# Cutting the first load of a key tile into three, in a one-core attention decode kernel

## The chip, the cores and the metric

The kernel runs on one core of a Trainium2 chip. The metric is the device time of one execution in microseconds (us); lower is better. A run is repeated, and the median is given with the lowest and the highest.

The names in this document are those of the profile. PE is the matrix engine (TensorE), and PEld its weight load. DVE is VectorE, ACT is ScalarE, POOL is GpSimd, SP is SyncE. A small q behind a name (SPq, DVEq) means the engine's sequencer, which issues transfers, waits and branches. The transfers themselves are made by 16 DMA engines that run side by side. Memory on the core (SBUF) has 128 partitions.

## What is computed

One query position attends to 65536 keys. There are 32 query heads and 8 heads of keys and values, so 4 query heads share one head of keys and values.

```python
B, Hq, Hkv, Sq, Sk, D = 1, 32, 8, 1, 65536, 128        # all in bf16
k = jnp.repeat(k, rep, axis=1)                          # rep = 4
v = jnp.repeat(v, rep, axis=1)
scores = jnp.einsum("bhqd,bhkd->bhqk", q, k) * D ** -0.5
p = softmax(scores, axis=-1)
return jnp.einsum("bhqk,bhkd->bhqd", p, v)
```

Keys and values are 268 MB together, and each of their bytes is used once for 4 query heads.

## The kernel before, in words

**Tiles.** A head's 65536 keys are laid on the 128 partitions, 512 rows (keys) to a partition. A row is 128 numbers of 2 bytes, so 256 bytes. A tile is half of a head: `NT = 256` rows in each partition, 64 KB in each partition and 8.4 MB together. There are 32 tiles, 16 of keys and 16 of values. The buffer `buf` holds three of them as a ring.

**Loads.** All tiles come in through SP. The helper `load` (L132, its transfer is on L134) writes one tile, or a part of its rows, into place `at % 3` of the ring, always in all 128 partitions. The order is written out by hand in the list `tiles` (L151 to L154): four tiles of keys, then values, then keys two heads ahead of the values. The first three loads wait for nothing; the first of all (L140) is issued ahead of everything else that SP does, before the start-up barrier that the profile books on L147, and the second on L150 behind it. From the fourth on SP first waits until the place is free (L162 to L167): for a key tile until PE or DVE has passed it, for a value tile until PE has used it. The last value tile comes in eight pieces (`PIECES`), so that little is left to do when the last byte has come. Every load adds 16 to a semaphore of its own place or piece when it has landed, one for each DMA engine. Loads on SP go through one queue, q1 in the profile.

**The query.** ACT loads q (8 KB, L222) through its own queue, q10. DVE transposes it (L298), PE multiplies it (L434), ACT copies it (L224), and POOL spreads it into the weights of the first head (L203).

**Keys.** For each head DVE takes a landed key tile (`turn`, L302; the wait is a `take` of the tile's semaphore, booked on L219) and transposes it in place in four steps (L308). PE multiplies the steps against the query's weights into four banks of scores (L453), with a `clear` (L411) ahead of each bank.

**Values.** DVE takes the maximum of the scores (L358), ACT makes the exponentials (L239), DVE transposes them (L313), and PE multiplies them with the rows of the value tiles (L477). PE runs the tiles as a loop with branches, not as straight code.

**DVE's start.** Before the first tile DVE makes small constant tables out of an identity matrix that POOL writes (L279 to L295): `rep`, `quad`, `sel`, `each`, then `rows4` (L287), then `away` (L292); then it waits for q (L297) and transposes it (L298). The tables and q's transpose are what PE waits for at its first instruction (L433).

**The end.** PE works through the last pieces (L530, L542), ACT scales the result (L252) and stores it.

Of the kernel before, what the change touches and what calls it, by code (L numbers as in the profile page):

```python
# [15 lines left out]
P = 128  # L16
D = 128
NT = 256
# [3 lines left out]
BY = {  # L22
    (G - 2, 0): (NT,), (G - 2, 1): (128, 128), (G - 1, 0): (128, 128),
}
N = 2
FAR = 2.0 ** 126
STEP = 32
# [5 lines left out]
def kernel(  # L33
# [24 lines left out]
    pe, dve, act, pool, sp = nc.tensor, nc.vector, nc.scalar, nc.gpsimd, nc.sync  # L58
    half = NT * D
    ring = 3 * half  # L60

    def sbuf(name, shape, dtype=fp32):
        return nc.alloc_sbuf_tensor(name, list(shape), dtype)
# [4 lines left out]
    buf = sbuf("buf", (P, ring), bf16)  # L68
# [27 lines left out]
    def sem(name):  # L96
        sems.append(nc.alloc_semaphore(name))
        return sems[-1]

    sK = [sem(f"sK{b}") for b in range(3)]  # L100
    sC, sD = sem("sC"), sem("sD")
    sL = [sem(f"sL{x}") for x in range(sum(map(len, BY.values())))]
    sP = [sem(f"sP{x}") for x in range(len(PIECES))]
    sQ = sem("sQ")
    sV = sem("sV")
    kt = sem("kt")
    clr = sem("clr")
# [21 lines left out]
    kr = [k[0, g].rearrange("(p n) d -> p (n d)", p=P) for g in range(G)]  # L129
    vr = [v[0, g].rearrange("(p n) d -> p (n d)", p=P) for g in range(G)]  # L130

    def load(at, src, s, lo=0, n=NT):  # L132
        at = at % 3 * half + lo * D
        return sp.dma_start(  # L134
            out=buf[:, at:at + n * D], in_=src[:, s * half + lo * D:s * half + (lo + n) * D]
        )

    first = load(0, kr[0], 0)  # L140
    tc.no_tile_sem_insts.add(first.ins.name)
    first.then_inc(sK[0], 16)
    tc.add_to_no_dep_group("first", first.ins)
    tc.declare_fence(pool.nop().ins, group="first")
    home = nc.cur_bb.parent
# [1 line left out]
    tc.compile()  # L147


    load(1, kr[0], 1).then_inc(sK[1], 16)  # L150
    tiles = [("k", 0, 0), ("k", 0, 1), ("k", 1, 0), ("k", 1, 1), ("v", 0, 0)]  # L151
    for g in range(2, G):
# [3 lines left out]
    for at, (kind, h, s) in enumerate(tiles):  # L156
        if at < 2:
            continue
        if at > 2:
            was, wh, ws = tiles[at - 3]  # L160
            if was == "k":
                sp.wait_ge(*((kb, wh + 1) if ws else (clr, 4 * wh + 3)))  # L162
            else:

                if (wh, ws) not in BY:
                    sp.wait_ge((sC, sD)[ws], 16 * (wh + 1)).then_inc(sV, NT // STEP)
                sp.wait_ge(vit, NT // STEP * (2 * wh + ws + 1))  # L167
        if kind == "k":
            load(at, kr[h], s).then_inc(sK[at % 3], 16)
        elif (h, s) == (G - 1, 1):  # L170
            lo = 0
            for n, land in zip(PIECES, sP):
                load(at, vr[h], s, lo, n).then_inc(land, 16)
                lo += n
        elif (h, s) in BY:
            lo = 0
            for n in BY[h, s]:
                load(at, vr[h], s, lo, n).then_inc(lands.pop(0), 16)
                lo += n
        else:  # L180
            load(at, vr[h], s).then_inc((sC, sD)[s], 16)
# [7 lines left out]
        out=ident[:, :], in_=ident[:, :], compare_op=ALU.not_equal, fill=1.0,  # L189
# [8 lines left out]
    for g in range(G):  # L198
        if g == 0:
            pool.wait_ge(qxs, 1)  # L200
        else:
            pool.wait_ge(outs, g)
        pool.tensor_tensor(  # L203
            out=wv[:, :, :, 0:H],
# [12 lines left out]
    def take(engine, semaphore, n=1):  # L217

        engine.wait_ge(semaphore, n).then_inc(semaphore, -n)  # L219
# [5 lines left out]
        out=qx[:, :].rearrange("p (b r h) -> p b h r", b=2, r=2),  # L225
        in_=misc[:, 0:P].rearrange("p (b h r) -> p b h r", b=2, r=2),
# [9 lines left out]
    for g in range(G + 1):  # L236
        if g < G:
            act.wait_ge(nms, g + 1)
            act.activation(  # L239
                out=E[:, :], in_=sc[:, :], func=ACT.Exp, bias=nmb[:, 0:1], scale=SCALE,  # L240
# [4 lines left out]
        at = max(g - 1, 0) * D  # L245
        act.activation(  # L246
            out=o_out[:, at:at + D], in_=psum_f[0:H, 0:D], func=ACT.Copy, scale=rl
# [5 lines left out]
        out=o_out[:, 0:D], in_=misc[0:H, 0:D], func=ACT.Copy, scale=rl_next  # L253
# [5 lines left out]
    def value(reg, below):  # L259
        return bass.RuntimeValue.of_register_unchecked(reg, min_val=0, max_val=below - 1)  # L260

    def moved(ap, by):

        return bass.AP(ap.tensor, ap.offset + by, ap.ap)
# [7 lines left out]
    def select(out, pattern, **at):  # L272

        return dve.tensor_reduce(
            out=out[:, :], in_=ident[:, :].rearrange(pattern, **at), axis=AX.X, op=ALU.max
        )
# [3 lines left out]
        out=rep.rearrange("p (a x) -> p a x", a=4),  # L280
        in_=ident[0:32, 0:32].unsqueeze(1).broadcast_to([32, 4, 32]),
    )
    select(quad, "p (a x) -> p a x", a=4)
    select(sel, "p (x h) -> p h x", h=H)
    select(each, "p (x h) -> p x h", h=H)

    dve.tensor_copy(  # L287
        out=rows4[:, :].rearrange("k (y d) -> k y d", y=4),
        in_=ident[0:4, 0:4].unsqueeze(2).broadcast_to([4, 4, D]),
# [3 lines left out]
        out=away.rearrange("k (q z r h) -> k z q r h", q=4, z=2, r=4)[:, 0],  # L293
# [5 lines left out]
        out=qt.bitcast(fp32), in_=qn.bitcast(fp32)  # L299
    ).then_inc(cst, 1)  # L300

    def turn(b):  # L302

        take(dve, sK[b], 16)
        for x in range(4):
            at = b * half + x // 2 * (half // 2)
            kv = buf[:, at:at + half // 2].bitcast(fp32).rearrange("p (c y e) -> p c y e", c=C, y=2)[:, :, x % 2]
            dve.transpose(out=kv, in_=kv).then_inc(kt, W // 2 // N)  # L308

# [45 lines left out]
    with block("turned"):  # L355
# [6 lines left out]
            out=same[:, :].rearrange("p (x h) -> p x h", h=H),  # L362
# [37 lines left out]
    def counter(name, below):  # L400

        reg = pe.alloc_register(name)
        return reg, value(reg, below)
# [3 lines left out]
    def add(reg, n, op=ALU.add):  # L407
        pe.reg_alu(reg, reg, n, op)
# [9 lines left out]
    def column(row):  # L418

        return 4 * (row // W * W + W - 1 - row % W)  # L420
# [8 lines left out]
    r_s, s = counter("s", 4 * W)  # L429
# [16 lines left out]
    with block("scores"):  # L446
        bank = sc[:, ds(value(r_x, 4) * 512, 512)]
        slide = value(r_s, 4 * (W - N) + 1)
        keys = value(r_p, ring - half // 2 + (W - N) * D + 1)
        take(pe, kt)  # L450
        for y in range(4 * N):
            m, n = y % 4, y // 4
            pe.matmul(  # L453
                out=bank,
# [3 lines left out]
            )  # L458
        add(r_p, N * D)
        add(r_s, 4 * N)  # L460
        pe.br_lt(s, 4 * W, on_true="scores", on_false="bank_end")
# [10 lines left out]
    with block("values"):  # L472
# [3 lines left out]
        for j in range(STEP // 4):  # L476
            last = pe.matmul(  # L477
                out=psum_o[0:16, :], lhsT=moved(Ew[:, column(4 * j + 3):][:, 0:16], weight),
# [14 lines left out]
    with block("summed"):  # L493
# [4 lines left out]
            out=misc[:, :], lhsT=same[:, :], rhs=each[:, :].unsqueeze(1).broadcast_to([P, 16, 32]),  # L498
# [22 lines left out]
    with block("tail"):  # L521
        at = sum(PIECES[:MOVED])
# [3 lines left out]
        for n, land in left[:1]:  # L526
            pe.wait_ge(land, 16)
            for row in range(at, at + n, 4):
                qd = row // 4 % 4 * 32
                pe.matmul(  # L530
                    out=psum_o[qd:qd + 16, :], lhsT=Ew[:, final + column(row + 3):][:, 0:16],
# [4 lines left out]
        for y, (n, land) in enumerate(left[1:]):  # L536
# [4 lines left out]
            for row in range(at, at + n):  # L541
                last = pe.matmul(  # L542
                    out=misc[0:H, 0:D], lhsT=Ew[:, final + column(row):][:, 0:H],
# [43 lines left out]
```

## Time and profile before

| | before |
|---|---|
| device time, median of 3 runs | 627.55 us (627.42 to 627.79) |
| device time of the profiled execution | 627.28 us |
| its span, first to last instruction | 625.4 us |
| PE busy | 510.1 us (82%) |
| DVE busy | 332.3 us (53%) |
| queue q1's packets, share of 16 DMA engines | 99.4% |

The span is what the profile sees of one execution; 627.28 - 625.4 = 1.9 us lie around it. Busy times of different engines overlap and can't be added. The share of q1 is the time that its packets took, divided by the span of 16 engines. A transfer's time "to landing" counts from its issue, so it holds the time that it stood in the queue behind earlier ones.

### The profile page before, as it was taken

How to read it: one execution, taken by the hardware profiler on the slowest of the kernel's cores; microseconds unless marked ns; L12 is line 12 of the kernel's file. 1: busy time of each engine (PE TensorE's matmuls, PEld its weight loads, DVE VectorE, ACT ScalarE, POOL GpSimd, SP SyncE). 2: the span in 40 equal slices, each digit the busy share in tenths (PEclk: the TensorE clock that was granted, in tenths of full speed). 3: DMA queues.
4: the chain of work that ended last, by engine and by line, in shares of the span. 5: the costliest groups of instructions: out<-in, count | busy, mean ns of one | idle time of the engine just before them, and what ended most of it. 6: DMA issues, size and time to landing. Idle time of an engine off the chain costs nothing. (4 is left out here: it accounts for less than half of the span.)

```text
span 625.4 us, 8105 instructions
## 1 busy us (share of the span) xinstructions
PE 510.1 (82%) x2186; PEld 203.7 (33%) x2186; DVE 332.3 (53%) x141; ACT 21.1 (3%) x28; POOL 6.0 (1%) x16
## 2 busy tenths in 40 slices
PE   0289499899995989939899398993899938999998
PEld 0034133333331333313333133331343313333333
DVE  2588897789214892148821588215872168721100
ACT  1000100100010000100001000010000100001000
POOL 2000000000000000000000000000000000000000
PEclk9998699899998989979999799996989969999999
DMA  9999999999999999999999999999999999999998
GB/s 403 402 469 402 469 402 469 402 469 402 461 411 428 444 411 461 402 469 402 469 402 469 402 469 402 444 428 411 461 402 469 402 469 402 469 402 436 430 410 335
DMA packets 5993, 268.46 MB, mean 429 GB/s; under 512 B 744, under 2 KB 1000, under 8 KB 1128
## 3 DMA queue, kind: packets, MB, share of 16 engines
q1 hardware_dynamic: 5904, 268.44, 99.4%
q10 hardware_dynamic: 88, 0.02, 0.0%
q14 instruction: 1, 0.01, 0.0%
HBM read 268.44 MB, written 0.01 MB: 429 GB/s over the span
## 5 line engine op out<-in xcount | busy, mean ns | idle before, releaser
L308 DVE STREAM_TRANSPOSE buf<-buf 128x4096 f32<-128x4096 f32 x64 | 278.7, 4413 | 119.1 <-DVEq L219 119.1
L453 PE MATMUL sc<-buf,zeros 128*128 x1024 | 255.4, 400 | 73.6 <-PEq L219 72.6
L477 PE MATMUL psum_o<-buf,Ew 128*16 x1008 | 223.7, 379 | 8.3 <-PEq L219 7.9
L453 PEld LDWEIGHTS sc<-buf,zeros 128*128 x1024 | 102.2, 100 | 219.7 <-issue 133.3
L477 PEld LDWEIGHTS psum_o<-buf,Ew 128*16 x1008 | 88.7, 88 | 139.9 <-issue 50.2
L321 DVE TENSOR_REDUCE o_r<-psum_o 128x128 f32<-128x512 f32 x10 | 6.8, 682 | 96.3 <-DVEq L219 69.6
L239 ACT ACTIVATE zeros<-sc,nmb 128x2048 bf16<-128x2048 f32 x8 | 15.7, 1967 | 535.2 <-DVE nmb L372 535.2
L313 DVE STREAM_TRANSPOSE Ew<-zeros 128x1024 bf16<-128x1024 bf16 x18 | 22.2, 1236 | 13.8 <-PE psum_o L477 13.8
L317 DVE COPY o_r<-o_r 4x1 f32<-4x1 f32 x9 | 1.3, 142 | 50.2 <-DVEq L219 37.2
L411 PE MATMUL sc<-zeros 128*128 128x512 bf16 x32 | 12.7, 398 | 11.4 <-PEq L219 8.1
L358 DVE TENSOR_REDUCE mx<-sc 128x1 f32<-128x2048 f32 x8 | 18.1, 2269 | 0.0
L497 PE MATMUL misc<-each,same 128*128 128x512 f32 x18 | 10.5, 669 | 5.5 <-PEq L219 5.5
L434 PE MATMUL misc<-Ew 32*128 32x128 bf16 x1 | 0.3, 282 | 13.2 <-DVE Ew L298 13.2
L411 PEld LDWEIGHTS sc<-zeros 128*128 128x128 bf16 x32 | 3.1, 96 | 20.5 <-issue 19.3
L203 POOL TENSOR_TENSOR zeros<-qx,quad 128x64 bf16<-128x64 bf16 x8 | 2.3, 294 | 482.4 <-ACT o_out L246 473.7
L414 PE MATMUL sc<-zeros 128*128 128x1 bf16 x32 | 5.2, 163 | 0.0
L411 PE MATMUL psum_o<-rows,zeros 4*128 4x512 bf16 x10 | 4.5, 446 | 0.6 <-PEq L219 0.6
L497 PEld LDWEIGHTS misc<-each,same 128*128 128x128 f32 x18 | 2.7, 188 | 5.8 <-issue 5.7
L279 DVE CAST Ew<-ident 32x128 bf16<-32x128 f32 x1 | 3.0, 2985 | 2.7 <-POOL ident L188 2.7
L434 PEld LDWEIGHTS misc<-Ew 32*128 32x128 bf16 x1 | 0.1, 98 | 13.2 <-DVE Ew L298 13.2
L414 PEld LDWEIGHTS sc<-zeros 128*128 128x128 bf16 x32 | 3.0, 95 | 3.9
L246 ACT ACTIVATE o_out<-psum_f,o_r 4x128 bf16<-4x128 f32 x9 | 3.1, 345 | 27.9 <-DVE o_r L327 27.9
(32 smaller groups left out, 35.8 us busy)
## 6 DMA issues: line engine op xcount, KB each, us to landing
buf<-in_v_dram SPq DMA_DIRECT2D x4, 4096.0 KB, 33.0
buf<-in_v_dram SPq DMA_DIRECT2D x2, 2048.0 KB, 31.2
buf<-in_v_dram SPq DMA_DIRECT2D x2, 1024.0 KB, 36.5
buf<-in_v_dram SPq DMA_DIRECT2D x1, 1408.0 KB, 40.4
buf<-in_v_dram SPq DMA_DIRECT2D x1, 288.0 KB, 40.7
buf<-in_k_dram SPq DMA_DIRECT2D x16, 36.0
buf<-in_v_dram SPq DMA_DIRECT2D x1, 224.0 KB, 40.8
buf<-in_v_dram SPq DMA_DIRECT2D x13, 35.6
```

Of the source, the lines that this page charges most:

```text
L239: act.activation(out=E[:, :], in_=sc[:, :], func=ACT.Exp, bias=nmb[:, 0:1], scale=SCALE, accum_out=o_r[:, D:D + 1],).then_inc(exd, 1)
L246: act.activation(out=o_out[:, at:at + D], in_=psum_f[0:H, 0:D], func=ACT.Copy, scale=rl).then_inc(outs, 1)
L279: dve.tensor_copy(out=rep.rearrange("p (a x) -> p a x", a=4), in_=ident[0:32, 0:32].unsqueeze(1).broadcast_to([32, 4, 32]),)
L308: dve.transpose(out=kv, in_=kv).then_inc(kt, W // 2 // N)
L313: return dve.transpose(out=Ew[:, at], in_=E[:, at])
L321: return dve.tensor_reduce(out=o_r[:, 0:D], in_=psum_o[:, :].rearrange("p (y d) -> p d y", y=4), axis=AX.X, op=ALU.max)
L358: after(dve.tensor_reduce(out=mx[:, :], in_=sc[:, :], axis=AX.X, op=ALU.max))
L411: return pe.matmul(out=bank, lhsT=lhsT, rhs=rhs, start=True, stop=False)
L414: return pe.matmul(out=bank[:, 0:1], lhsT=zer[:, 0:P], rhs=zer[:, 0:1], start=False, stop=True)
L453: pe.matmul(out=bank, lhsT=moved(wq[:, m * SLIDE + 4 * n:][:, 0:P], slide), rhs=moved(T[:, n, m // 2, m % 2], keys), start=False, stop=False,)
L477: last = pe.matmul(out=psum_o[0:16, :], lhsT=moved(Ew[:, column(4 * j + 3):][:, 0:16], weight), rhs=moved(buf[:, 4 * j * D:][:, 0:4 * D], ...
L497: pe.matmul(out=misc[:, :], lhsT=same[:, :], rhs=each[:, :].unsqueeze(1).broadcast_to([P, 16, 32]), start=True, stop=True,).then_inc(pes, 1)
```

## The change

The first load is cut into three transfers. The first brings 64 of the 256 rows of the first tile, in the first 16 partitions only (`HEAD = 16`): 16 times 16 KB. It keeps its place ahead of the start-up barrier. The second brings the other 192 rows of these 16 partitions, 16 times 48 KB. The third brings all 256 rows of the other 112 partitions, 112 times 64 KB. The second and the third are issued where the second tile's load stood, ahead of it. The first two report to a new semaphore, `sF`; the third reports to `sK[0]`, which the whole tile's load used to do. DVE waits for both reports on `sF` ahead of making `rows4`, and so before it takes the first tile.

```diff
+HEAD = 16
...
-    sQ = sem("sQ")
+    sQ, sF = sem("sQ"), sem("sF")
...
-    def load(at, src, s, lo=0, n=NT):
+    def load(at, src, s, lo=0, n=NT, part=slice(0, P)):
         at = at % 3 * half + lo * D
         return sp.dma_start(
-            out=buf[:, at:at + n * D], in_=src[:, s * half + lo * D:s * half + (lo + n) * D]
+            out=buf[part, at:at + n * D], in_=src[part, s * half + lo * D:s * half + (lo + n) * D]
         )
...
-    first = load(0, kr[0], 0)
+    first = load(0, kr[0], 0, 0, 64, slice(0, HEAD))
     tc.no_tile_sem_insts.add(first.ins.name)
-    first.then_inc(sK[0], 16)
+    first.then_inc(sF, 16)
...
+    load(0, kr[0], 0, 64, NT - 64, slice(0, HEAD)).then_inc(sF, 16)
+    load(0, kr[0], 0, part=slice(HEAD, P)).then_inc(sK[0], 16)
     load(1, kr[0], 1).then_inc(sK[1], 16)
...
     select(each, "p (x h) -> p x h", h=H)
+    dve.wait_ge(sF, 32)
 
     dve.tensor_copy(
         out=rows4[:, :].rearrange("k (y d) -> k y d", y=4),
```

## The prediction

> **What bounds the kernel now.** I read the page's head first, then the DMA slices and the queue table: is any engine as full as the transfers?
>
> ```profile
> span 625.4 us, 8105 instructions
> ...
> PE 510.1 (82%) x2186; PEld 203.7 (33%) x2186; DVE 332.3 (53%) x141; ACT 21.1 (3%) x28; POOL 6.0 (1%) x16
> ...
> DMA  9999999999999999999999999999999999999998
> ...
> q1 hardware_dynamic: 5904, 268.44, 99.4%
> ```
>
> No. The 16 DMA engines are at 90% or more in 39 of 40 slices, and the packets of q1 fill 99.4% of their time; PE is busy for 82% and DVE for 53%. Next, whether anything holds the transfers up: SP's own waits, the issue of the fourth load in SP's timeline, and the end of the chain of waits.
>
> ```profile
> SPq L134 <- PE sc L411: 219.9, 8, 42.2
> SPq L134 <- PE psum_o L477: 195.6, 13, 19.5
> ```
>
> ```profile
> 45.00 0.33 SPq L134 DMA_DIRECT2D buf<-in_k_dram  x1
> ```
>
> ```profile
> 581.01 40.38 DMA buf<-in_v_dram
> 621.39 0.04 issue
> 621.44 0.82 PE psum_o L530 x11
> ```
>
> SP waits 219.9 us in all for PE to free places of key tiles, which looks like a bound and isn't one, as the issue at 45.00 us will show. The chain ends in 40.38 us of a last piece under way, and PE starts on it at once: the last byte sets the end. Now the rate, from two windows; the last column is GB/s.
>
> ```profile
> 1.00:21.00 20.00, 1.32 (x3) 0.23 (x3) 3.58 (x7) 2.01 (x2) 3.74 (x5) 1.00 1.01 420
> ...
> 24.00:624.00 600.00, 508.81 (x2183) 203.49 (x2183) 327.39 (x134) 18.94 (x26) 2.06 (x7) 0.94 1.00 432
> ```
>
> The steady rate is 432 GB/s. I call one partition's 64 KB of a tile a *strip*. Sixteen strips, one on each DMA engine, are 1.049 MB and take 1.049 / 432 = **2.43 us**, one strip-time. A tile is 8 strip-times, 19.4 us. Three tiles last until about 60 us, so the load issued at 45.00 us comes some 15 us early. And since the stream is full from then on, a microsecond lost near its start is a microsecond of the result.
>
> **The change part by part.** First the issues, and when bytes begin to move.
>
> ```profile
> 0.74 0.37 SPq L134 DMA_DIRECT2D buf<-in_k_dram  x1
> ```
>
> ```profile
> 1.89 0.88 SPq L134 DMA_DIRECT2D buf<-in_k_dram  x2
> ```
>
> ```profile
> 1.00:2.00 1.00, 0.00 (x0) 0.00 (x0) 0.00 (x0) 0.00 (x0) 0.10 (x1) 1.00 2.81 918
> ```
>
> *The small first load.* It is issued at 0.74 us as before. Packets are booked where they begin, so the 918 GB/s says that the whole load's first strips begin between 1.00 and 2.00 us. A load of 16 KB on each engine could begin sooner. The gain lies between nothing and 2.00 - 0.74 = 1.26 us, and I take nothing, as the row shows no part of that time that depends on the size. The load holds 0.262 MB, 0.61 us at full rate. The next load is issued 1.89 - 0.74 = 1.15 us after it, behind the barrier, so the engines can run dry for up to 1.15 - 0.61 = 0.54 us. I take nothing here too, because that is less than the uncertainty of the large terms; both ends go into the range.
>
> *Two more issues on SP.* Two took 0.88 us, so the second tile's load is issued 0.88 us later, near 2.8 us. The first tile covers that, since it occupies the engines for 19.4 us; without that cover it would cost the 0.88 us. SP's first wait comes later still.
>
> *The head: 16 partitions on 16 engines.* The first two loads together are one strip for each engine, so they would take one strip-time if only the engines counted. But look where the bytes go. In all loads of before, a partition gets its 64 KB of a tile in 19.4 us: 3.4 GB/s, the highest lasting rate that any partition shows here. To lose nothing, 16 partitions would have to take in 64 KB each in 2.43 us: eight times that. The trace has no large load into fewer than 128 partitions, so it can't say whether engine, memory or receiving side makes the 432 GB/s. Bounds: at eight times the shown rate the head takes 1 strip-time, and at just the shown rate it takes 8. The extra is 0 to 7 strip-times; I take the middle, **3.5**, since no row is nearer to one end.
>
> [...]
>
> *The other 112 partitions.* Each engine has 7 strips to bring in place of the remaining 7 of 8, so nothing is added as long as the engines don't meet. In the full loads they evidently don't: 16 strips go on at 432 GB/s whatever their order. With 128 partitions, 8 to an engine fit any grouping by eights, fours or twos; with 112 partitions from number 16 on, 7 to an engine don't. If two engines send to one group in the same strip-time, both go at half speed and a strip-time is lost. The bounds are 0 and 7, one for each of the 7 strips; I take the middle again, **3.5**.
>
> [...]
>
> *DVE's new wait.* Queued behind it are `rows4`, `away`, q's transpose and the first tile; PE, ACT and POOL wait for the third of these.
>
> ```profile
> 3.48 2.43 DVE L287 CAST rows<-ident 4x512 bf16<-4x512 f32 x1
> 5.84 0.17 DVE L292 TENSOR_SCALAR zeros<-ident 4x64 bf16<-4x64 f32 x1
> 12.88 0.23 DVE L298 STREAM_TRANSPOSE Ew<-Ew 32x64 f32<-32x64 f32 x1 [6.87 <-DMA Ew<-in_q_dram]
> 22.67 17.43 DVE L308 STREAM_TRANSPOSE buf<-buf 128x4096 f32<-128x4096 f32 x4 [9.56 <-DVEq L219]
> ```
>
> ```profile
> 15.20 0.61 PE L411 MATMUL sc<-zeros 128*128 128x512 bf16 x1 [1.32 <-PEq L219]
> ```
>
> If the first strips begin by 2.00 us, the head has landed by 2.00 + 4.5 x 2.43 = 12.9 us. Behind it stand 2.43 + 0.17 + 0.23 us on DVE, and from the transpose's end at 13.11 us to PE's first score clear 15.20 - 13.11 = 2.1 us: 4.9 us, done at 17.8 us. The third load follows the head with at least 7 strip-times, 17.0 us, so the tile is complete no sooner than 29.9 us and covers all of it, with 12 us to spare. If the cover were gone, the 4.9 us would come into the path. q itself takes turns with slower strips and may land later than 12.88 us; the same cover holds for it.
>
> *What is late next.* A tile that lands 17 us later moves DVE, PE and the issues behind it by the same 17 us; the 15 us by which the fourth load comes early stay as they are, because both sides move. The end of the chain is the same.
>
> **Sum**, against the profiled execution (627.28 us, span 625.4, 1.9 us around it, 0.27 us below the median of 627.55): 627.28 + (3.5 + 3.5) x 2.43 = 627.28 + 17.0 = **644.3 us**.
>
> **The rivals.**
>
> *The third load fits after all.* Engines that meet fall out of step and then pass each other. In its favour: 15 us of early issue lets a fast engine run ahead into the next tile. [...] 627.28 + (3.5 + 1) x 2.43 = 638.2 us; with a head of 1 extra, 632.1.
>
> *No receiving limit: the split costs nothing.* The engines or the memory make the 432 GB/s. In its favour: the engines are booked as full in each window. Against it: it needs the eightfold rate in the head. 627.3 to 627.8 us with the dry 0.54 us; I take 627.5.
>
> *Faster: the start gets shorter.* The small first load is prepared quickly and bytes move at once, up to 1.26 us sooner. The first window's 420 instead of 432 GB/s is a further 20 x 12 / 432 = 0.56 us of slow start. 627.28 - 1.82 = 625.5 us at best. It decides only if the head loses under half a strip-time, and it needs both gains nearly whole to pass 0.2%.
>
> *Engines meet in almost each strip of the third load.* 627.28 + (3.5 + 7) x 2.43 = 652.8 us, and 661.3 with the head at its worst.
>
> *The loads don't do what they say* (a load on fewer engines, say): 16 and 112 partitions both divide by the 16 engines, so I give it no chance of its own.
>
> **How the numbers follow.** Four doublings lead from the shown rate of a partition to the eightfold: once, twice, four and eight times. Only the last loses nothing in the head, one case in four; and the third load must lose nothing as well, about one in two. That leaves 0.14, of which 0.02 is the faster case and 0.12 no change. The rest: forecast 0.49, the third load that fits 0.32, the worst case 0.05. Chances: faster by over 0.2% 0.02, within 0.2% 0.12, slower by over 0.2% 0.86; 0.2% (1.3 us) is about what a measurement of this kernel can tell from no change. The range takes the first two cases, from 2 strip-times (632.1) to 10 (651.6); outside are 0.19.
>
> **What would show it.** In the changed profile, the first window of 1 to 12 us should show far less than 420 GB/s, near 1.05 MB in some 11 us; the steady rate later should again be 432, and the first key transposes should start near 40 us instead of 22.67. If the first window keeps 420 and the transposes start near 22.7, the receiving side limits nothing and the forecast is wrong at its root. If the head is slow and the transposes start near 33, the third load fits. If q's transpose moves and the first key transposes start later than the tile's landing, DVE's wait was not covered.

## The result, and the profile after

| | before | after |
|---|---|---|
| device time, median | 627.48 us (627.33 to 627.80, 6 runs) | 648.79 us (648.54 to 648.99, 6 runs) |
| device time of the profiled execution | 627.28 us | 648.97 us |
| its span | 625.4 us | 647.1 us |

The ratio is 1.034, with a 95% interval of 1.0329 to 1.0351. The change costs 648.79 - 627.48 = **21.3 us**; 17.0 were forecast. The time lies in the stated range.

The page of the changed kernel first: its span, the instructions by engine, the DMA slices and the queue of the loads.

```profile
span 647.1 us, 8107 instructions
...
PE 509.5 (79%) x2186; PEld 203.6 (31%) x2186; DVE 332.4 (51%) x141; ACT 21.1 (3%) x28; POOL 6.0 (1%) x16
...
DMA  9989999999999999999999999999999999999997
GB/s 195 243 275 446 446 405 446 446 405 446 450 401 446 454 405 438 454 429 421 446 446 405 446 446 405 446 450 401 446 454 405 438 454 429 417 450 415 429 420 300
...
q1 hardware_dynamic: 5952, 268.44, 99.2%
```

The engines do the same work: PE's busy time is 509.5 us where it was 510.1, DVE's 332.4 where it was 332.3. Now put the two DMA lines together (a busy digit 9 is 90% or more). The busy digits stay at eight or nine from the first slice to the last but one, and q1 is again above 99%, so by busy share nothing has happened. The GB/s under it tell where the time went: 195, 243 and 275 in the first three slices (16 us each), and the usual 400 to 454 from the fourth on, but for the last. The first slice, at 195 GB/s, has the same digit 9 as the fourth, at 446: a packet counts as busy time for as long as it takes. The share shows that the queue is never empty, not that the engines move bytes at their rate.

The windows of the changed kernel put edges to that (the last column is GB/s).

```profile
2.00:12.00 10.00, 0.00 (x0) 0.00 (x0) 2.98 (x4) 1.28 (x1) 3.34 (x4) 1.00 1.26 186
12.00:32.00 20.00, 1.32 (x3) 0.23 (x3) 0.75 (x3) 0.72 (x1) 0.29 (x1) 1.00 0.99 249
44.00:624.00 580.00, 488.12 (x2069) 194.80 (x2069) 328.01 (x133) 18.76 (x25) 2.04 (x7) 0.94 1.00 433
```

After 44 us the rate is 433 GB/s, as it was (432). All of the loss lies in the first tile, and most of it in the part after 12 us, which holds nearly nothing but the third load. Next the first transfers, as the page lists them: size, then the time from issue to landing.

```profile
buf<-in_k_dram SPq DMA_DIRECT2D x1, 768.0 KB, 10.3
...
buf<-in_k_dram SPq DMA_DIRECT2D x1, 256.0 KB, 4.7
```

And DVE's timeline of the changed kernel, which answers to the rows shown of before:

```profile
12.27 0.41 DVE L291 CAST rows<-ident 4x512 bf16<-4x512 f32 x1 [6.61 <-DMA buf<-in_k_dram]
12.61 0.17 DVE L296 TENSOR_SCALAR zeros<-ident 4x64 bf16<-4x64 f32 x1
17.05 0.23 DVE L302 STREAM_TRANSPOSE Ew<-Ew 32x64 f32<-32x64 f32 x1 [4.27 <-DMA Ew<-in_q_dram]
44.51 17.42 DVE L312 STREAM_TRANSPOSE buf<-buf 128x4096 f32<-128x4096 f32 x4 [27.23 <-DVEq L222]
```

The new wait is there: DVE stands idle for 6.61 us until the head lands, and resumes at 12.27 us. Then come q at 17.05 us and, after 27.23 us of waiting for the first tile, the key transposes at 44.51 us instead of 22.67. That is 21.8 us later, the whole loss. The rest moves with it: the fourth load's issue, from SP's timeline, and the end of the chain.

```profile
66.84 0.33 SPq L135 DMA_DIRECT2D buf<-in_k_dram  x1
```

```profile
602.67 40.37 DMA buf<-in_v_dram
643.04 0.04 issue
643.09 0.82 PE psum_o L534 x11
```

66.84 - 45.00 = 21.8 us and 643.09 - 621.44 = 21.7 us: both have moved by as much as the first tile, and nothing of it is won back.

### The profile page after: what moved, and what is told of

It reads as the page before. It is cut to its first block, busy times and chain, and to the rows that moved or that the text cites. A ratio compares the mean times of both kernels' runs of the same rounds, so it can differ in the third digit from the quotient of the medians.

```text
span 647.1 us, 8107 instructions
## 1 busy us (share of the span) xinstructions
PE 509.5 (79%) x2186; PEld 203.6 (31%) x2186; DVE 332.4 (51%) x141; ACT 21.1 (3%) x28; POOL 6.0 (1%) x16
## 6 DMA issues: line engine op xcount, KB each, us to landing
buf<-in_k_dram SPq DMA_DIRECT2D x1, 768.0 KB, 10.3
```

## The experiments

The theories are guesses of the author, and the runs are to decide between them. Theory A: the receiving side is the limit; the 16 DMA engines would keep their rate only while they write into different groups of neighbouring partitions, and where several meet at one group, they would share its rate. The rivals: B, the cut itself costs (more issues, DVE's wait); C, a single partition takes in only so much; D, the memory side is slow on these source strips; E, any load narrower than 128 partitions is slow, wherever its partitions lie.

Eleven of the twelve runs use one method, so that a load can be timed without touching the first tile's: the kernel before with one load *more*, ahead of all others, into the ring's third place. Nothing reads those bytes, and the third tile's load, which overwrites them, waits for them. The stream is full behind it, so the time that the load takes from the stream is read off the end of the kernel. The kernel before, measured beside them, has medians of 627.59, 627.47 and 627.43 us; each difference below is taken from the one that belongs to the run.

The trace also holds a record of every packet: when it begins, how long it takes, its size, but not its engine. A load that brings 64 KB to each partition has one packet of 64 KB for each, so a strip is one packet. In the first 60 us of the kernel before, 16 packets of 64 KB are under way at once for 96% of the time, and the next one mostly begins where one ends; by that the strips are put in order below.

**Only the cut, over all partitions.** Against the changed kernel:

```diff
-HEAD = 16
+HEAD = P
...
-    load(0, kr[0], 0, 64, NT - 64, slice(0, HEAD)).then_inc(sF, 16)
-    load(0, kr[0], 0, part=slice(HEAD, P)).then_inc(sK[0], 16)
+    load(0, kr[0], 0, 64, NT - 64, slice(0, HEAD)).then_inc(sK[0], 16)
...
-    dve.wait_ge(sF, 32)
+    dve.wait_ge(sF, 16)
```

> The first load is cut by rows alone: 64 rows of all 128 partitions ahead of the barrier, then the other 192 rows of all 128 partitions; DVE still waits for the first part ahead of rows4. Theory A (the receiving side charges for few partitions): nothing is lost, 627.5 us within 0.6. Theory B (the cut, the extra issues or DVE's wait cost the time): a good part of the 21.3 us stays, above 632 us.

Measured 627.37 us against 627.59; the ratio is 0.9996 (0.9987 to 1.0005). The window and DVE's timeline of this kernel:

```profile
1.00:21.00 20.00, 1.31 (x3) 0.23 (x3) 3.65 (x7) 2.01 (x2) 3.73 (x5) 1.00 1.00 420
```

```profile
8.04 0.41 DVE L290 CAST rows<-ident 4x512 bf16<-4x512 f32 x1 [2.40 <-DMA buf<-in_k_dram]
8.39 0.18 DVE L295 TENSOR_SCALAR zeros<-ident 4x64 bf16<-4x64 f32 x1
8.49 0.23 DVE L301 STREAM_TRANSPOSE Ew<-Ew 32x64 f32<-32x64 f32 x1
22.56 17.43 DVE L311 STREAM_TRANSPOSE buf<-buf 128x4096 f32<-128x4096 f32 x4 [13.85 <-DVEq L221]
```

DVE waits for the first part here too (2.40 us), and it costs nothing: 420 GB/s and transposes at 22.56 us, as before. Rival B falls. What costs is that the loads are cut by partitions.

**The head alone, and the same bytes spread out.**

```diff
...
-    first = load(0, kr[0], 0)
+    first = sp.dma_start(
+        out=buf[0:16, 2 * half:3 * half], in_=kr[0][0:16, 0:half]
+    )
...
-    first.then_inc(sK[0], 16)
+    first.then_inc(sF, 16)
...
+    load(0, kr[0], 0).then_inc(sK[0], 16)
     load(1, kr[0], 1).then_inc(sK[1], 16)
+    sp.wait_ge(sF, 16)
```

> The kernel before with one load more, ahead of all others: 64 KB into each of partitions 0 to 15, in the ring's third place, from the first 16 of the key rows' strips; the third tile's load waits for it. Nothing reads it. 1.05 MB more. Theory A: the 16 neighbours take in a quarter of the full rate, so it costs 4 strip-times, 9.7 us, about 637.2 us. If the engines alone set the rate: 1 strip-time, 2.4 us, about 629.9 us.

Measured 636.59 us, 9.0 us more than the kernel before. From here on each edit is shown against this run, that of e5_x112_src against e4_x112.

```diff
-        out=buf[0:16, 2 * half:3 * half], in_=kr[0][0:16, 0:half]
+        out=buf[0:P:8, 2 * half:3 * half], in_=kr[0][0:16, 0:half]
```

> As e2_x16, with the same bytes from memory, written to partitions 0, 8, 16 and so on to 120 instead of 0 to 15. Theory A, with entries shared by neighbouring partitions: clearly less than e2_x16, 2 strip-times, 4.9 us, about 632.4 us. Rival C (each partition has a slow rate of its own) and rival D (the memory side is slow on these source strips): the same as e2_x16, about 637.2 us.

Measured 632.50 us, 4.9 us more. The same 16 strips from the same places in memory, into as many partitions, cost about half when they are spread out. Rivals C and D don't allow that; theory A, with groups of neighbours that share one entry, does.

**The source changed, the partitions kept.**

```diff
-        out=buf[0:16, 2 * half:3 * half], in_=kr[0][0:16, 0:half]
+        out=buf[0:16, 2 * half:3 * half], in_=kr[0][0:P:8, 0:half]
```

> As e2_x16 (16 neighbouring partitions, 636.6 us), into the same partitions, but from source strips 0, 8, 16 and so on to 120. Theory A: unchanged, 636.6 us. Rival D (memory side): like e3_x16_far or otherwise, 632.5 us or less.

Measured 636.93 us, 9.5 us more, against 9.0 in e2_x16. It is no faster: the memory side doesn't set the head's time.

**The other 112 partitions alone.**

```diff
-        out=buf[0:16, 2 * half:3 * half], in_=kr[0][0:16, 0:half]
+        out=buf[16:P, 2 * half:3 * half], in_=kr[0][16:P, 0:half]
```

> The kernel before with one load more, ahead of all others: 64 KB into each of partitions 16 to 127, in the ring's third place. 7.34 MB more, 7 strip-times, 17.0 us if the engines never meet: 644.5 us. If the third load of the change is slow by itself, as its landing 32 us behind the head suggests: 30 us or more, about 658 us. If it is slow only because it follows the narrow head: near 644.5 us.

Measured 659.43 us, 31.8 us more, where 17.0 would be 7 strip-times. The third load is slow by itself, and not as an after-effect of the head.

```diff
-        out=buf[16:P, 2 * half:3 * half], in_=kr[0][16:P, 0:half]
+        out=buf[16:P, 2 * half:3 * half], in_=k[0, 0].rearrange("(p n) d -> p (n d)", n=NT)[16:P, :]
```

> As e4_x112 (112 partitions, 659.4 us), into the same partitions, but the strips come from memory one right behind the other (64 KB apart instead of 128 KB). Theory A (engines meet on the receiving side): unchanged, 659.4 us. Rival D (the memory side is slow on strips at these distances): clearly another time, down to 644.5 us.

Measured 658.35 us. The ratio to the kernel before is 1.0494 (1.0477 to 1.0512), and that of e4_x112 1.0507 (1.0491 to 1.0523): no difference that these runs can tell. Rival D falls for the third load as well.

**Other widths.**

```diff
-        out=buf[0:16, 2 * half:3 * half], in_=kr[0][0:16, 0:half]
+        out=buf[32:P, 2 * half:3 * half], in_=kr[0][32:P, 0:half]
```

> One load more ahead of all others, into partitions 32 to 127: 6 strips for each engine. If two engines meet in each strip-time of any load that isn't 128 partitions wide, as the times of e4_x112 come out: 6 times 4.54 us, 27.2 us, 654.8 us. If 7 strips an engine is an odd count that only 112 has: 6 strip-times, 14.6 us, 642.2 us.

Measured 656.94 us, 29.5 us more: 4.9 us for each of 6 strips. The odd 7 is not the cause; the expected 27.2 us were even too few.

```diff
-        out=buf[0:16, 2 * half:3 * half], in_=kr[0][0:16, 0:half]
+        out=buf[0:64, 2 * half:3 * half], in_=kr[0][0:64, 0:half]
```

> One load more ahead of all others, into partitions 0 to 63: 4 strips for each engine. Theory A with neighbours sharing entries by halves: 4 times 4.54 us, 18.1 us, 645.7 us. If half the partitions are enough for the full rate: 4 strip-times, 9.7 us, 637.3 us.

Measured 647.94 us, 20.5 us more: 5.1 us for each of 4 strips, more than double.

**Does narrow mean slow?** After these runs rival E was still open, because nothing narrower than 128 partitions had been fast.

```diff
-        out=buf[0:16, 2 * half:3 * half], in_=kr[0][0:16, 0:half]
+        out=buf[0:32:4, 2 * half:3 * half], in_=kr[0][0:8, 0:half]
```

> One load more ahead of all others, 64 KB into each of 8 partitions: 0, 4, 8 and so on to 28. Theory A (it is slow only where engines meet at one group of neighbours): 8 partitions in 8 groups, nothing meets, 1 strip-time on the engines that take part, 2.4 us, 629.9 us. Rival E (any load narrower than 128 partitions goes at half rate or less, wherever its partitions lie): 4.6 us or more, 632.1 us or above.

```diff
-        out=buf[0:16, 2 * half:3 * half], in_=kr[0][0:16, 0:half]
+        out=buf[0:8, 2 * half:3 * half], in_=kr[0][0:8, 0:half]
```

> As e9_x8_far, into partitions 0 to 7 instead. Theory A with groups of four: 8 partitions in 2 groups, 4 engines at each, 9.0 us as in e2_x16, 636.5 us. Rival E: the same as e9_x8_far.

Measured 631.95 us (e9_x8_far, 4.5 more) and 636.13 us (e10_x8, 8.7 more). The second is as theory A has it. The first is not decided by its time, which is nearer to rival E's 632.1 than to 629.9. The trace's packet records decide: the 8 strips took 2.8 to 3.3 us, as the first strips of the kernel before do (2.9 to 3.4), while those of e10_x8 took 7.8 to 8.8 us. So these 8 strips were not slowed. Part of what was added is the issue: this load's takes longer, and the next issue is late (SP's timeline of e9_x8_far):

```profile
0.73 0.77 SPq L140 DMA_DIRECT2D buf<-in_k_dram  x1
2.59 3.65 SPq L134 DMA_DIRECT2D buf<-in_k_dram  x3
```

0.77 us instead of 0.37, and the tile's load at 2.59 us instead of 1.89, 0.7 us late. With 2.4 us for the strip that explains 3.1 of the 4.5 us. The packet records show where the other 1.4 arise: two of the eight engines begin their next strip only 0.8 and 1.0 us after the end of the first, take 3.5 us for it, and stay some 1.5 us behind the others, and the stream ends with its last engine. Why these two lag stays open.

```diff
-        out=buf[0:16, 2 * half:3 * half], in_=kr[0][0:16, 0:half]
+        out=buf[0:P:4, 2 * half:3 * half], in_=kr[0][0:32, 0:half]
```

> One load more ahead of all others, into 32 partitions: 0, 4, 8 and so on to 124, 2 strips for each engine. If the number of groups that a load reaches sets its rate: all are reached, 2 strip-times, 4.9 us, 632.4 us. If it is which engines meet at one time: two at a group, 2 times 4.54 us, 9.1 us, 636.6 us.

Measured 632.64 us, 5.2 us more: 2.6 us for each of 2 strips. This load has a quarter of the partitions and runs at nearly the full rate. Rival E falls. The windows from 2 to 12 us of three kernels show it: 32 partitions four apart, then 64 neighbours, then 16 neighbours.

```profile
2.00:12.00 10.00, 0.71 (x2) 0.13 (x2) 3.58 (x7) 1.72 (x2) 3.44 (x4) 1.00 1.05 420
```

```profile
2.00:12.00 10.00, 0.00 (x0) 0.00 (x0) 3.35 (x6) 1.28 (x1) 3.44 (x4) 1.00 1.18 249
```

```profile
2.00:12.00 10.00, 0.00 (x0) 0.00 (x0) 3.35 (x6) 1.28 (x1) 3.35 (x4) 1.00 0.63 138
```

The last column is 420, 249 and 138 GB/s. The column ahead of it, the DMA share, is 1.05, 1.18 and 0.63, and doesn't follow the rate: packets are booked where they begin (1.18 is more than the window's whole time of 16 engines), and a slow one that begins ahead of the window is left out.

**The control.**

```diff
-        out=buf[0:16, 2 * half:3 * half], in_=kr[0][0:16, 0:half]
+        out=buf[0:P, 2 * half:3 * half], in_=kr[0][0:P, 0:half]
```

> The control: one load more ahead of all others, into all 128 partitions, 8 strips for each engine. All theories: 8 strip-times, 19.4 us, 646.9 us. Another time would mean that the method itself (a load more, a wait ahead of the third tile's load) costs something.

Measured 646.82 us, 19.4 us more, as expected to 0.1 us. The method adds nothing of its own.

The packet records give the middle time of a 64 KB strip, in the order in which the 16 engines send them (of 8 engines in the two rows of 8 partitions):

```text
load                            strip 1     2     3     4     5     6     7
whole tile (before)                3.22  2.42  2.42  2.42  2.42  2.42  2.42
112, partitions 16 to 127          4.35  4.55  3.15  4.05  4.49  4.59  4.55
96, partitions 32 to 127           4.45  5.11  4.80  5.08  4.83  5.11
64, partitions 0 to 63             4.74  5.12  5.13  5.12
32, partitions 0, 4, ... 124       3.19  2.42
16, partitions 0 to 15             8.54
16, partitions 0, 8, ... 120       4.66
8, partitions 0 to 7               8.22
8, partitions 0, 4, ... 28         3.06
```

The first strip of a kernel holds about 0.8 us of starting up (3.22 against 2.42). The row of 112 hides one thing: in the third strip two of the 16 engines took 4.8 and 4.9 us, and they come out of the load 0.9 and 1.7 us behind the middle one. Later, in the stream of whole tiles, the middle engine of e4_x112 is 13.0 us late beyond its 7 strips, the last one 14.6 us.

## Why the prediction was right

**What bounds the kernel**: right. The steady rate is the same to 1 GB/s, the fourth load's issue moved by as much as the first tile, and the loss at the start is the loss at the end.

**The small first load and the two issues**: right to cost them at nothing. e1_rows_all keeps a first load of a quarter of the rows, one of the two issues more and the wait, and is within 0.1% of the kernel before. Its first load is eight times as large as that of the change, so it doesn't test the time in which the engines run dry; the sum of the large terms, below, leaves nothing for that. The faster rival had no start to win: in the packet records the first strips begin at 1.73 us before and 1.76 us after. (The row of 918 GB/s holds 0.918 MB, 14 of the 16 first strips and not all of them; the last begins at 2.07 us.)

**The head**: that the receiving side holds it up is right, and its size was a little high; the bound behind it was misread. 3.4 GB/s is what a partition gets on average over the 19.4 us of a tile. In the packet records of the kernel before, each partition's 64 KB come in one packet of 2.42 us, so at 27 GB/s: the eightfold rate, which the prediction took as never shown, was there in every load. A single partition was no limit, and the upper bound of 8 strip-times had no ground in the row that it was read from; nor had the chance of one in four that was worked out from the doublings. What limits is shared by neighbours, as e2_x16 against e3_x16_far shows (9.0 against 4.9 us). That the middle, 3.5, came out near the measured extra is luck.

3.5 strip-times of extra, 8.5 us, were forecast. e2_x16 gives 636.59 - 627.59 = 9.0 us for the head in all, of which 2.4 are the strip-time that it saves elsewhere: 6.6 us, 2.7 strip-times. DVE resumed at 12.27 us, where the landing was expected by 12.9. In the trace the head lasts from 1.76 us, where its first packet begins, to its landing at 1.90 + 10.3 = 12.2 us: 10.4 us, where the forecast has 4.5 x 2.43 = 10.9. The last of its packets ends at 10.9 us, ahead of the landing.

**The third load**: this is the term that was mis-sized. It was forecast at 3.5 strip-times of extra (8.5 us), as the middle of 0 and 7. e4_x112 gives 31.8 - 17.0 = **14.8 us, 6.1 strip-times**. Half of the strips were expected to take double. By the table five of the seven took 1.7 to 1.9 times 2.42 us, the first, without its start-up, 1.5 times and the third 1.3 times. All in all the middle engine loses 13.0 us, and most of the rest of the 14.8 us is that the stream waits for the engines that fell behind in the third strip, for which the prediction has no term. The reason given, that 7 strips to an engine fit no grouping, isn't borne out either: 6 strips, and 4, which do fit a grouping by fours or twos, ran no faster (e7_x96, 4.9 us a strip; e8_x64, 5.1). That two engines which send to one group go at half speed was the author's assumption; no run shows which engines sent where.

The two measured terms together, 6.6 + 14.8 = 21.4 us, give the 21.3 us of the change, and leave nothing for other causes, within the 1 us or so that the intervals of e2_x16 and e4_x112 allow. In the forecast the two misses partly cancel: the head was 1.9 us too high, the third load 6.3 us too low. That the sum was off by only 4.3 us is in part luck.

**DVE's wait**: right. It delays `rows4` by 12.27 - 3.48 = 8.8 us, and 27.23 us of waiting for the first tile cover it. The work behind it was read wrong in part: `rows4` took 0.41 us there and not 2.43, and q's transpose waited for q until 17.05 us, so that PE's first clear of scores began at 19.37 us, where 17.8 was expected. The cover takes that in as well, as the prediction says of a late q.

**The rivals.** "The third load fits after all" was given 0.32 and is refuted by e4_x112; the 1 strip-time that its sum adds for this load is shown by no run, and e4_x112 gave 6.1. "Engines meet in almost each strip" was given 0.05, and for the third load it is nearly what happens; a head smaller by 1.9 us and a third load of 6.1 strip-times and not 7 (2.2 us) keep the time at 648.8 and not 652.8 us. "The split costs nothing" is true of e1_rows_all, and only there.

**The signs.** The first window is far below 420 GB/s, as was said:

```profile
1.00:12.00 11.00, 0.00 (x0) 0.00 (x0) 2.98 (x4) 1.28 (x1) 3.44 (x4) 1.00 1.25 191
```

191 GB/s in 11 us are 2.1 MB, though, and not 1.05: the third load's first strips begin from 9.4 us on and are booked there. The steady rate came as said, and the key transposes later than the 40 us that were expected, at 44.51 us.

**What stays open.** Why 112 or 96 neighbouring partitions are at about half rate (31.8 us where 7 strip-times are 17.0, and 29.5 us where 6 are 14.6) isn't settled. The number of partitions doesn't order the loads: the second strip took 2.42 us with 32 partitions four apart, 5.12 us with 64 neighbours and 4.55 us with 112. The author's guess is that it matters which engines write where at one time; no run shows that. Which engine gets which partition of such a load wasn't measured, so that the meeting of engines fits the narrow loads (8.54 us for a strip into 16 neighbours, 4.66 us into 16 spread out) and is only argued for the wide ones.

## What to carry to other kernels

Cut a load by rows, not by partitions: a cut over all 128 partitions cost nothing here, and 16 + 112 partitions cost 8.8 strip-times of the stream. Look at GB/s beside the busy share of the DMA engines: here the busy digits stood at eight and nine over 195 to 275 GB/s, as they did over 446. Where a kernel is a full stream from end to end, time any disputed load by adding it in front and reading the end; the control came out to 0.1 us.

## What the runs showed of the hardware that was not expected

- The narrow load of e10_x8 slowed engines that have no part in it. Its eight strips go to partitions 0 to 7; in the packet records eight more, which begin beside them from 3.6 us on and so belong to the other eight engines and the whole-tile load, took 8.0 us for a strip (middle value) as well, and 2.9 us beside the spread load of e9_x8_far. In the 112-partition load, too, most engines slow down together: 14 of 16 took 2.8 to 3.4 us in the third strip, and all of them 3.88 us or more in the fourth.
- The strips of the slowed wide loads settle near double: 4.55 us (112 partitions) and 5.12 us (64 partitions), against 2.42 us in the kernel before. Two strips in these times are 28.8 and 25.6 GB/s, against 27.1 GB/s for one strip in 2.42 us (65.5 KB): as if two engines had the rate of one between them. What they would share isn't shown.
- Loads differ in the time that SP takes to issue them: 0.54 us (four apart, 32 partitions), 0.57 us (eight apart) and 0.77 us (four apart, 8 partitions), where most loads into neighbours took 0.37 to 0.39 us. Spacing alone isn't the reason: the load into 64 neighbours (e8_x64) took 0.54 us as well. What sets the time stays open.
